# Attention and two mixture layers on one core: order of GpSimd's and TensorE's work within a head step

## The chip, the cores and the metric

The kernel runs on one core of a Trainium2 chip. What is measured is the time of one execution on the device in microseconds (us). TensorE is called PE, its weight loads PEld, VectorE DVE, ScalarE ACT, GpSimd POOL and SyncE, which issues most transfers, SP.

## The reference

Three layers follow one another: attention that keeps the 32 largest scores of each row, a gated layer of width 2048 (called the first layer here, as the kernel's `mm1` and `mm2` are its two products), and a mixture of eight experts with two per token.

```python
scores = q @ k.T / sqrt(64)                       # 4 batches, 8 heads, 576 x 576
kth = the 32nd largest score of each row
attn = softmax(where(scores >= kth, scores, -1e9))
x = attn @ v                                      # 2304 tokens x 512
h = x @ w_in;  x = (h * clip(h + 3, 0, 6) / 6) @ w_out   # w_in 512 x 2048, w_out 2048 x 512, float64
logits = x @ w_gate + log1p(exp(x @ w_noise)) * noise     # the two best of 8 experts
out = sum over the two: weight * (max(x @ w1[e], 0) @ w2[e])
```

## The kernel before, in words

The function `phase_a` does attention, the gated layer and the routing, `phase_b` the experts. Phase A is one long software pipeline over *steps* `st`. A slot is one head for one tile of 128 tokens; there are 144 slots (18 tiles by 8 heads). In each step every stage works on another slot: `scores` of slot st-1, the segment maxima (`seg`) of st-1, the chain that finds the 32nd value (`chain`) and the bias for the exponential (`nbias`) of st-2, `ysum` and `expo` of st-3, `ymax` and `pmask` of st-4, the transposes `ptrans` of st-5, and the products with V (`av`) for a pair of heads, in odd steps, when its second slot is st-6. From step 25 on each step also does one unit of the gated layer: `mm1` of unit u with `hrelu` and `hgate`, and for the unit of the step before (`up`) `hround`, `hlow` and `mm2`. `hlow` makes the lower half of the split value g, on POOL.

The normalisation of a head pair takes three small operations: `recip1` (POOL adds 1e-9 to the two row sums), `recip2` (DVE takes the reciprocal) and `recip3` (POOL spreads the two values over 128 columns, tile `rb`). `av` ends with a transpose of `rb` on PE into the same PSUM bank as the products; ACT copies that bank out two steps after (`xscale`, tile `xs`) and POOL multiplies (`xscale2`).

In the first 21 steps the float64 weights are also converted (`Weights.convert`): DVE shifts bits, ACT scales the low words, and POOL adds the two in place. The order of the first 21 steps is chosen by the framework's scheduler. From step 22 (`KEEP`) on, PE, DVE, ACT and POOL run what `phase_a` issues in exactly the order in which it is written, each engine in its own queue. The routing's indirect transfers (`idw`, 12 for each of the first two groups of tiles) are issued by POOL and are placed by the scheduler, each behind a given `hlow`. Further loads that POOL and ACT share a part of: `q_split` (lower half of q, tile `qsb`) in every second even step, and `k_split` (tile `ksb`) in eight steps ahead of each batch.

Names in the rows: `sum` is the pair of row sums, `a` the bias, `xs`, `xT` the attention values, `g` and `y` as above, `s`, `h`, `pa`, `qp`, `xa`, `av` PSUM banks of scores, `mm1`, `ptrans`, transposed q, `mm2`, and products with V, `e` the exponentials. A helper issues everything in phase A, so all its rows have line 87.

Of the kernel before, what the change touches and what calls it, by code (L numbers as in the profile page):

```python
# [13 lines left out]
ALU = mybir.AluOpType  # L14
# [21 lines left out]
OS, OA, OB, OC, OD, OE, OV, OX, OY = 1, 1, 2, 3, 4, 5, 6, 8, 10  # L36
# [24 lines left out]
def pieces(t):  # L61
    r0 = t * 128
    res = []
    row = 0
    while row < 128:
        b, s = divmod(r0 + row, S)
        n = min(128 - row, S - s)
        res.append((b, row, n, s))
        row += n
    return res  # L70
# [39 lines left out]
class Weights:  # L110
# [27 lines left out]
    def convert(self, fb):  # L138


        if not self.f64:
            return
        nc, t = self.nc, self.raws[fb]
        if self.small:
            m = self.ap.tile([128, 1024], F32, name=f"wm{fb}", tag="wm", bufs=1)
            nc.vector.tensor_scalar(m.bitcast(I32), t[:, :, 1], 0x7FFFFFFF, None, op0=ALU.bitwise_and)
            nc.vector.tensor_scalar(m, m, TINY, None, op0=ALU.is_ge)
        for i in range(2):
            hi = t[:, 512 * i:512 * i + 512, 1]
            tmp = self.ap.tile([128, 512], I32, name=f"wt{fb}_{i}", tag="lx", bufs=LXB)  # L150
            nc.vector.tensor_scalar(tmp, hi, 3, 0x3FFFFFF8, op0=ALU.logical_shift_left, op1=ALU.bitwise_and)
            nc.vector.scalar_tensor_tensor(hi, hi, -0x40000000, tmp, op0=ALU.bitwise_and, op1=ALU.bitwise_or)
        lo = t[:, :, 0]
        nc.scalar.activation(lo, lo.bitcast(U32), AF.Copy, scale=2.0 ** -29)
        nc.gpsimd.tensor_tensor(t[:, :, 1], t[:, :, 1], t[:, :, 0], op=ALU.add)
        if self.small:

            nc.vector.tensor_tensor(t.bitcast(F32)[:, :, 1], t.bitcast(F32)[:, :, 1], m, op=ALU.mult)
# [18 lines left out]
def phase_a(tc, pools, ident, q, k, v, w_in, w_out, X, worst, wscr, stream, begin, on_chunk=None, slots=NSLOT, pace=None):  # L177
    nc = Lanes(tc)
# [35 lines left out]
    def w_split(fb):  # L214
        if fb in stream:
            w = wp.tile([128, 2, 1024], F32R, name=f"wsp{fb}", tag="ws", bufs=NSTR)
        else:
            w = wp.tile([128, 2, 1024], F32R, name=f"w{fb}", tag="wr", bufs=NRES)
            wres[fb] = w
        wk.split(fb, w, fb % 16 < WP)  # L220
        if fb in stream:
            nc.sync.dma_start(wscr[fb], w.bitcast(F32))

    def copy(kind, out, in_):
        (nc.vector.tensor_copy if kind in ONV else nc.scalar.copy)(out, in_)
# [12 lines left out]
    def k_load(i):  # L238
        dl, b, h = ksched[i]
        KR[i] = kr = ap.tile([128, 5, 64], F32, name=f"kr{i}", tag="kr", bufs=KRB)  # L240
        nc.sync.dma_start(kr[:, 0:4, :], k[b, h, 0:512, :].rearrange("(p j) d -> p j d", j=4))
        nc.sync.dma_start(kr[0:64, 4, :], k[b, h, 512:576, :])

    def k_split(i):

        kr = KR.pop(i)
        KS[i] = ks = ksb[i % KSB]
        for sl in ((slice(0, 128), slice(0, 4)), (slice(0, 64), slice(4, 5))):
            hi, lo = ks[sl[0], sl[1], 0, :], ks[sl[0], sl[1], 1, :]
            copy('k', hi, kr[sl])  # L250
            nc.gpsimd.tensor_tensor(lo, kr[sl], ks.bitcast(F32)[sl[0], sl[1], 0, :], op=ALU.subtract)
# [44 lines left out]
    def q_load(t, g):  # L296
        QR[t, g] = qr = ap.tile([128, 4, 64], F32, name=f"qr{t}_{g}", tag="qr", bufs=QRB)
        for (b, row, n, s0) in pieces(t):
            nc.sync.dma_start(qr[row:row + n], q[b, 4 * g:4 * g + 4, s0:s0 + n, :].rearrange("h s d -> s h d"))
# [50 lines left out]
    def seg(i, j):  # L350
        nc.vector.max(ST[i][:, j, :], SS[i][:, edge[j]:edge[j + 1]])
# [12 lines left out]
    def nbias(i):  # L364
        a = A8[i]
        nc.gpsimd.tensor_scalar(a[:, 24:25], a[:, 16:17], -0.125, 1.0, op0=ALU.mult, op1=ALU.mult)
# [45 lines left out]
    def recip1(p):  # L412
        nc.gpsimd.tensor_scalar(SUM[p], SUM[p], 1e-9, 1.0, op0=ALU.add, op1=ALU.mult)

    def recip2(p):
        nc.vector.reciprocal(SUM[p], SUM[p])

    def recip3(p):
        r = SUM.pop(p)
        rb = ap.tile([128, 2, 64], F32, name=f"rb{p}", tag="rb", bufs=2)  # L420
        nc.gpsimd.tensor_scalar(rb, r[:, :, None].to_broadcast([128, 2, 64]), 1.0, 1.0, op0=ALU.mult, op1=ALU.mult)
        RB[p] = rb
# [29 lines left out]
    def av(p):  # L452

        t = p // 4
        AVP[p] = o = ps.tile([128, 512], F32, name=f"av{p}", tag="av")
        for b, row, n, s0 in pieces(t):
            for j in range(5):
                for hh in (1, 0):
                    half = slice(64 * hh, 64 * hh + 64)
                    vt, pt = V[b, (2 * p + hh) % 8][:, j, :], PT[2 * p + hh][:, j, :] if j < 4 else PH[p]  # L460
                    nc.tensor.matmul(o[half, row:row + n], vt, pt[:, row:row + n], start=(j == 0),
                                     stop=(j == 4), skip_group_check=True)
        nc.tensor.transpose(o[:, 128:256], RB.pop(p).rearrange("p a b -> p (a b)"), ident)
# [6 lines left out]
    def xscale2(p):  # L470
        xs = XR.pop(p)
        nc.gpsimd.tensor_tensor(xs[:, 0:128], xs[:, 0:128], xs[:, 128:256], op=ALU.mult)
        XS[p] = xs[:, 0:128]
# [96 lines left out]
    for c, ts in enumerate(chunks):  # L570
        st = max(8 * ts[-1] + 7 + LAG, last + 1)
# [7 lines left out]
    ok = lambda i: 0 <= i < slots  # L579
# [4 lines left out]
    for st in range(-6, end):  # L584
        if st == -6: q_load(0, 0)
        if st == BEGIN: begin()
        if st == KEEP: nc.keep()
        if st % 4 == 0 and 0 < st // 4 + 1 < slots // 4: q_load(*divmod(st // 4 + 1, 2))
        for i, (dl, b, h) in enumerate(ksched):
            if max(dl - 4, min(i, 2) - 6) == st: k_load(i)  # L590
        for fb in wstep.get(st + 2, []): wk.load(fb)

        while fetched < len(units) and units[fetched][0] <= st + 3:
            w_fetch(units[fetched][1]); fetched += 1
        u, up = ustep.get(st), ustep.get(st - 1)
        s_, a, b, c, d, e, av_, x1, x2 = (st - x for x in (OS, OA, OB, OC, OD, OE, OV, OX, OY))
        ki = kdl.get(st)

        if up:
            hround(up)  # L600
            hlow(up)
        if ok(s_):
            scores(s_)
            s_evac(s_)
        if ok(c):
            ysum(c)
            expo(c)
        if ok(d - 1) and d % 2 == 0: recip1(d // 2 - 1)
        if u:
            mm1(u)  # L610
            hrelu(u)
        if ok(e):
            ptrans(e)
            ptevac(e)
        if ki is not None or ok(st):
            kq_trans(ki, st if ok(st) else None)
        if ok(st): q_evac(st)
        if ok(x1) and x1 % 2 == 0: xscale(x1 // 2)

        ch = chain(b) if ok(b) else []  # L620
        segs = [(a, j) for j in range(NSEG)] if ok(a) else []
        if ok(d): ymax(d)
        if ok(d - 1) and d % 2 == 0: recip2(d // 2 - 1)
        if ch:
            ch.pop(0)()
            nbias(b)
        while ch:
            if segs: seg(*segs.pop(0))
            ch.pop(0)()
        if segs: seg(*segs.pop(0))  # L630
        if u: hgate(u)
        if ok(b): zmask(b)
        if ok(d):
            pmask(d)
        while segs: seg(*segs.pop(0))

        if ok(d - 1) and d % 2 == 0: recip3(d // 2 - 1)
        if ok(x1) and x1 % 2 == 0: xscale2(x1 // 2)
        if up:
            mm2(up)  # L640
            if up[1] == NFB - 1: xout(up[0])
        if ki is not None:
            k_trans(ki)
            k_evac(ki)
        if ok(av_) and av_ % 2: av(av_ // 2)
        for i, (dl, b, h) in enumerate(ksched):
            if dl + VL == st: v_load(i)
        if ok(x2) and x2 % 2 == 0: xsplit(x2 // 2)
        if st % 4 == 2 and 0 <= st // 4 + 1 < slots // 4: q_split(*divmod(st // 4 + 1, 2))
        for i, (dl, b, h) in enumerate(ksched):  # L650
            if max(dl - 2, min(i, 2) - 5) == st: k_split(i)
        for fb in wstep.get(st, []): w_split(fb)
        for fb in wstep.get(st + 1, []): wk.convert(fb)
        room = NFILL if st < slots + OD else 3 * NFILL
        while fill and room > 0:
            room -= fill[0][0]
            fill.pop(0)[1]()
# [669 lines left out]
```

## Time and profile before

| | |
|---|---|
| runs | 1385.82 us median of 3 (1384.4 to 1390.74) |
| profiled execution | 1381.3 us, of which the span from first to last instruction is 1379.5 us |
| mean granted TensorE clock | 0.975 of full speed |
| busy in the span | PE 1293.2, PEld 1121.2, DVE 948.3, POOL 829.9, ACT 770.2 us |

The profiled execution is one of its own, 4.5 us (0.3%) below the median of the runs shown. Busy times are averages over stages that differ: the first 145 us (weights and first slots), the head steps up to about 810 us, and what follows on PE.

### The profile page before, as it was taken

How to read it: one execution, taken by the hardware profiler on the slowest of the kernel's cores; microseconds unless marked ns; L12 is line 12 of the kernel's file. 1: busy time of each engine (PE TensorE's matmuls, PEld its weight loads, DVE VectorE, ACT ScalarE, POOL GpSimd, SP SyncE). 2: the span in 40 equal slices, each digit the busy share in tenths (PEclk: the TensorE clock that was granted, in tenths of full speed). 3: DMA queues.
4: the chain of work that ended last, by engine and by line, in shares of the span. 5: the costliest groups of instructions: out<-in, count | busy, mean ns of one | idle time of the engine just before them, and what ended most of it. 6: DMA issues, size and time to landing. Idle time of an engine off the chain costs nothing. (4 is left out here: it accounts for less than half of the span.)

```text
span 1379.5 us, 27084 instructions
## 1 busy us (share of the span) xinstructions
PE 1293.2 (94%) x9006; PEld 1121.2 (81%) x9006; DVE 948.3 (69%) x3560; ACT 770.2 (56%) x1709; POOL 829.9 (60%) x1159
## 2 busy tenths in 40 slices
PE   5878899999999989999999899899999999999996
PEld 3554689989888878898988688788988898898985
DVE  7999987899987978869989753446353545435241
ACT  6888777777778666777777554534322322222220
POOL 7666777677767786767687845133324547465451
PEclk9789999999999999999999999999999999999999
DMA  7776644545365353445544447846446556465431
GB/s 249 261 279 226 230 145 157 193 166 176 132 206 166 127 149 124 170 131 187 175 143 157 123 154 246 265 140 221 136 153 195 178 167 204 140 214 177 137 109 38
DMA packets 138100, 239.56 MB, mean 174 GB/s; under 512 B 39779, under 2 KB 93155, under 8 KB 123872
## 3 DMA queue, kind: packets, MB, share of 16 engines
q1 hardware_dynamic: 127600, 210.57, 46.1%
q0 software_dynamic: 10352, 27.18, 5.9%
q8 instruction: 73, 1.20, 0.4%
q14 instruction: 75, 0.61, 0.2%
HBM read 209.08 MB, written 31.64 MB: 174 GB/s over the span
## 5 line engine op out<-in xcount | busy, mean ns | idle before, releaser
L959 PE MATMUL ac<-w,hh 128*128 128x512 f32 x960 | 247.8, 400 | 1.6 <-ACT hh L941 1.5
L935 PE MATMUL hb<-xe,w 128*128 128x320 f32 (+2 forms) x1536 | 239.4, 311 | 1.0 <-DVE hh L942 0.5
L935 PEld LDWEIGHTS hb<-xe,w 128*128 128x128 f32 x1536 | 232.1, 189 | 10.0 <-issue 3.9
L87 DVE MAX8 seg<-ss 128x8 f32<-128x82 f32 (+1 forms) x1008 | 213.9, 231 | 4.1 <-ACT ss L87 3.7
L87 POOL TENSOR_TENSOR y<-z,ss 128x576 f32<-128x576 bf16 x144 | 205.3, 1426 | 11.7 <-DVE z L87 10.1
L941 ACT ACTIVATE hh<-hb 128x640 fp32r<-128x640 f32 (+2 forms) x72 | 46.6, 647 | 295.7 <-PE hb L935 295.7
L959 PEld LDWEIGHTS ac<-w,hh 128*128 128x128 f32 x960 | 172.8, 188 | 40.3 <-ACT hh L941 5.4
L942 DVE SCALAR_TENSOR_TENSOR hh<-hb,hh 128x640 fp32r<-128x640 f32 (+2 forms) x72 | 53.9, 749 | 213.2 <-ACT hh L941 213.2
L87 PE MATMUL h<-xT,ws 128*128 128x256 f32 x1188 | 159.1, 283 | 9.3 <-DVE r L87 7.9
L87 ACT COPY ss<-s 128x576 f32<-128x576 f32 x144 | 92.6, 643 | 134.6 <-DVE e L87 69.6
L87 PE MATMUL xa<-ws,g 128*128 128x512 f32 x594 | 163.9, 410 | 2.2 <-POOL g L87 0.9
L87 PEld LDWEIGHTS h<-xT,ws 128*128 128x128 f32 x1188 | 150.0, 190 | 12.8 <-DVE r L87 9.9
L921 POOL TENSOR_TENSOR w<-r,w 128x1024 fp32r<-128x1024 f32 x40 | 97.9, 2452 | 85.2 <-ACT w L919 73.4
L87 DVE SCALAR_TENSOR_TENSOR e<-ss,t,e 128x576 f32<-128x576 f32 x144 | 147.6, 1025 | 0.1
L87 POOL TENSOR_TENSOR g<-r,g 128x256 fp32r<-128x256 f32 x124 | 100.2, 808 | 39.8 <-issue 19.6
L87 PEld LDWEIGHTS xa<-ws,g 128*128 128x128 f32 x594 | 104.0, 190 | 23.6 <-POOL g L87 5.1
L87 DVE TENSOR_SCALAR_CACHE_REDUCE z<-ss,a 128x576 bf16<-128x576 f32 x144 | 115.8, 804 | 0.2
L87 ACT ACTIVATE e<-ss,a 128x576 f32<-128x576 f32 x144 | 110.6, 768 | 1.4 <-POOL a L87 1.4
L87 PE MATMUL s<-kt,qt 128*128 128x288 f32 x512 | 101.2, 321 | 7.8 <-ACT qt L87 6.8
L87 DVE MAX8 t<-y 128x8 f32<-128x584 f32 x144 | 107.8, 749 | 0.0
L975 POOL DMA_INDIRECT out_dram<-y,id x40 | 41.8, 1045 | 108.9 <-DVE y L974 86.7
L87 PE MATMUL pa<-ident,e 128*128 128x128 f32 x576 | 91.3, 283 | 15.4 <-DVE e L87 13.4
(427 smaller groups left out, 2617.2 us busy)
## 6 DMA issues: line engine op xcount, KB each, us to landing
ws<-wscr SPq DMA_DIRECT2D x99, 1024.0 KB, 4.8
r<-in_moe_w_dram SPq DMA_DIRECT2D x144, 256.0 KB, 3.1
wscr<-wsp SPq DMA_DIRECT2D x11, 1024.0 KB, 5.8
wraw<-in_moe_w_in_dram SPq DMA_DIRECT2D x16, 512.0 KB, 4.2
wraw<-in_moe_w_out_dram SPq DMA_DIRECT2D x16, 512.0 KB, 5.1
ck<-in_moe_w_in_dram SPq DMA_DIRECT2D x32, 256.0 KB, 3.4
ck<-in_moe_w_out_dram SPq DMA_DIRECT2D x32, 256.0 KB, 3.2
out_dram<-zero SPq DMA_DIRECT2D x18, 256.0 KB, 4.2
```

The costliest lines, as they stand in the source:

```text
L87: o = f(*args, **kw)
L921: eng.tensor_tensor(w[:, 1], r, w.bitcast(F32)[:, 0], op=ALU.subtract)
L935: o = nc.tensor.matmul(p[:, half, 0:hn], w[:, a, d, :], XE[job][:, b, d, half * hn:(half + 1) * hn], start=(m == 0), stop=(m == 11))
L941: nc.scalar.activation(hv[:, 0], p[:, 0:nh, 0:hn], AF.Relu)
L942: LOW[:] = [STT(hv[:, 1], p[:, 0:nh, 0:hn], 0.0, h.bitcast(F32)[:, :, 0:n].rearrange("p a (b n) -> p a b n", b=nh)[:, 0], op0=ALU.max, op1 ...
L959: o = nc.tensor.matmul(ACC[job, j], h[:, a, j * 128:(j + 1) * 128], w[:, b, :], start=(x % NF2 == 0 and m == 0), stop=(x % NF2 == NF2 - 1 ...
L975: s = nc.gpsimd.indirect_dma_start(out=out, out_offset=bass.IndirectOffsetOnAxis(ap=t.bitcast(I32)[:, j, 1:2], axis=0), in_=y, in_offset=N ...
```

## The change

Four things are written in another order or another size; no arithmetic changes. (1) POOL's addition in `convert` is done in four pieces of 256 columns. (2) `recip2` moves in DVE's step from behind `ymax` to the end. (3) `recip3` moves from the end of the even step to the following odd step, behind `ysum`. (4) `nbias` moves to the end of POOL's part of the step, and `av` moves in front of `mm2`.

```diff
-        nc.gpsimd.tensor_tensor(t[:, :, 1], t[:, :, 1], t[:, :, 0], op=ALU.add)
+        for i in range(0, 1024, 256):
+            nc.gpsimd.tensor_tensor(t[:, i:i + 256, 1], t[:, i:i + 256, 1], t[:, i:i + 256, 0], op=ALU.add)
...
         if ok(d - 1) and d % 2 == 0: recip1(d // 2 - 1)
+        if ok(d - 2) and d % 2: recip3(d // 2 - 1)
         if u:
             mm1(u)
...
         if ok(d): ymax(d)
-        if ok(d - 1) and d % 2 == 0: recip2(d // 2 - 1)
         if ch:
             ch.pop(0)()
-            nbias(b)
...
         while segs: seg(*segs.pop(0))
-        if ok(d - 1) and d % 2 == 0: recip3(d // 2 - 1)
+        if ok(d - 1) and d % 2 == 0: recip2(d // 2 - 1)
         if ok(x1) and x1 % 2 == 0: xscale2(x1 // 2)
+        if ok(av_) and av_ % 2: av(av_ // 2)
         if up:
             mm2(up)
...
-        if ok(av_) and av_ % 2: av(av_ // 2)
...
             if max(dl - 2, min(i, 2) - 5) == st: k_split(i)
+        if ok(st - OB): nbias(st - OB)
```

On POOL, an even step and the following odd one (units 8 and 9 of a block of the gated layer) stand like this before:

```order
L87 TENSOR_TENSOR y_8598<-z_8557,ss_8419 128x576
L87 TENSOR_SCALAR sum_8477<-sum_8477 128x2
L87 TENSOR_SCALAR a_8636<-a_8636 128x1
L87 TENSOR_SCALAR rb_8657<-sum_8477 128x128
L87 TENSOR_TENSOR xs_8634<-xs_8634 128x128
L87 TENSOR_TENSOR xT_7971<-xs_8458,xT_7971 128x128
L87 TENSOR_TENSOR qsb_112<-qr_1_8407,qsb_112 128x4x64
L87 TENSOR_TENSOR g_9_8678<-r_9_8616,g_9_8678 128x256
L87 TENSOR_TENSOR y_8689<-z_8651,ss_8508 128x576
L87 TENSOR_SCALAR a_8721<-a_8721 128x1
```

And the same steps on POOL in the changed kernel:

```order
L87 TENSOR_TENSOR y_8646<-z_8604,ss_8467 128x576
L87 TENSOR_SCALAR sum_8523<-sum_8523 128x2
L87 TENSOR_TENSOR xs_8682<-xs_8682 128x128
L87 TENSOR_TENSOR xT_8016<-xs_8506,xT_8016 128x128
L87 TENSOR_TENSOR qsb_112<-qr_1_8455,qsb_112 128x4x64
L87 TENSOR_SCALAR a_8684<-a_8684 128x1
L87 TENSOR_TENSOR g_9_8724<-r_9_8664,g_9_8724 128x256
L87 TENSOR_TENSOR y_8735<-z_8697,ss_8554 128x576
L87 TENSOR_SCALAR rb_8740<-sum_8523 128x128
L87 TENSOR_SCALAR a_8769<-a_8769 128x1
```

The bias `a` now stands behind `qsb`, directly ahead of the next `g`, and `rb` has moved from ahead of `xs` to behind the odd step's `g` and `y`.

On PE, the odd step of that pair before (ten products with V, of which the first and the last stand here):

```order
L87 MATMUL h_10_8694<-xT_6467,ws_10_8409 128x256 x12
L87 MATMUL qpNone_8716<-identr,qsb_111 128x128 x2
L87 MATMUL xa_7963<-w_1219,g_9_8678 128x512 x3
L87 MATMUL xa_7967<-w_1219,g_9_8678 128x512 x3
L87 MATMUL av_8747<-pt_8627,v_7246 64x128
...
L87 MATMUL av_8747<-ph_8625,v_7159 64x128
L87 MATMUL av_8747<-ident,rb_8657 128x128
L87 MATMUL s_8770<-kt_6464,qt_8719 128x288 x4
```

And in the changed kernel:

```order
L87 MATMUL h_10_8742<-xT_6512,ws_10_8457 128x256 x12
L87 MATMUL qpNone_8764<-identr,qsb_111 128x128 x2
L87 MATMUL av_8788<-pt_8675,v_7291 64x128
...
L87 MATMUL av_8788<-ph_8673,v_7206 64x128
L87 MATMUL av_8788<-ident,rb_8740 128x128
L87 MATMUL xa_8008<-w_1247,g_9_8724 128x512 x3
L87 MATMUL xa_8012<-w_1247,g_9_8724 128x512 x3
L87 MATMUL s_8818<-kt_6509,qt_8767 128x288 x4
```

The products with V and the transpose of `rb` now stand between the transposed q and the second product of the gated layer, which with the next scores is queued behind them.

On DVE, from the end of an odd step into the even one, before:

```order
L87 SCALAR_TENSOR_TENSOR e_8334,sum_8477<-ss_8243,t_8115,e_8334 128x576
L87 MAX seg_8510<-ss_8508 128x8 x2
L87 MAX t_8115<-y_8511 128x8
L87 RECIPROCAL sum_8477<-sum_8477 128x2
L87 MAX a_8636<-seg_8510 128x8
L87 MAX seg_8597<-ss_8595 128x8
```

And in the changed kernel, the end of the even step:

```order
L87 TENSOR_SCALAR z_8697,low<-ss_8554,a_8684 128x576
L87 SCALAR_TENSOR_TENSOR e_8560,sum_8699<-ss_8374,t_8163,e_8560 128x576
L87 MAX seg_8645<-ss_8643 128x8 x2
L87 RECIPROCAL sum_8523<-sum_8523 128x2
L87 MAX t_8163<-y_8646 128x8
```

The reciprocal of the same pair now comes almost a whole step later on DVE, behind that step's `hgate`, `z` and `e`.

## Rows read from the trace of the kernel before

**Rows 1.** Busy time in four stretches: start:end, length, PE PEld DVE ACT POOL, PEclk, DMA, GB/s

```profile
50.00:100.00 50.00, 37.65 (x241) 26.78 (x240) 49.28 (x186) 42.09 (x87) 33.85 (x45) 0.86 0.76 269
300.00:350.00 50.00, 50.00 (x414) 45.09 (x413) 45.40 (x211) 36.42 (x92) 34.10 (x52) 1.00 0.49 164
1050.00:1100.00 50.00, 49.91 (x283) 44.58 (x282) 21.88 (x43) 13.72 (x18) 25.36 (x17) 1.00 0.48 155
```

**Rows 2.** Waits from 150 to 800 us: waiter, releaser: us in total, times, longest

```profile
DVE sum L87 <- POOL sum L87: 89.0, 60, 4.8
POOL xs L87 <- ACT xs L87: 67.9, 54, 2.4
...
PEld xa L87 <- POOL g L87: 6.0, 17, 1.3
```

**Rows 3.** Timeline, PE, scores two steps apart: start, us, instruction [idle before <-releaser]

```profile
291.14 0.69 PE L87 MATMUL s<-kt,qt 128*128 128x288 f32 x4
...
300.69 0.56 PE L87 MATMUL s<-kt,qt 128*128 128x288 f32 x3
```

**Rows 4.** Timeline, POOL, a pair of steps with q_split

```profile
308.91 0.30 POOL L87 TENSOR_SCALAR rb<-sum 128x128 f32<-128x128 f32 x1
...
311.19 1.25 POOL L87 TENSOR_TENSOR qsb<-qr,qsb 128x256 fp32r<-128x256 f32 x1
312.40 0.73 POOL L87 TENSOR_TENSOR g<-r,g 128x256 fp32r<-128x256 f32 x1
313.09 1.30 POOL L87 TENSOR_TENSOR y<-z,ss 128x576 f32<-128x576 bf16 x1
314.36 0.20 POOL L87 TENSOR_SCALAR a<-a 128x1 f32<-128x1 f32 x1
```

**Rows 5.** Timeline, PE's weight loads, the odd step of that pair

```profile
312.70 0.30 PEld L87 LDWEIGHTS xa<-ws,g 128*128 128x128 f32 x2
313.18 0.77 PEld L87 LDWEIGHTS xa<-ws,g 128*128 128x128 f32 x4 [0.19 <-POOL g L87]
314.31 0.85 PEld L87 LDWEIGHTS av<-pt,v 128*64 128x64 f32 x16 [0.37 <-issue]
...
315.56 0.14 PEld L87 LDWEIGHTS av<-ident,rb 128*128 128x128 f32 x1 [0.17 <-issue]
```

**Rows 6.** Timeline, DVE, the even step of that pair

```profile
308.40 0.17 DVE L87 RECIPROCAL sum<-sum 128x2 f32<-128x2 f32 x1 [0.48 <-POOL sum L87]
...
310.98 0.86 DVE L87 SCALAR_TENSOR_TENSOR e<-ss,t,e 128x576 f32<-128x576 f32 x1
```

**Rows 7.** Timeline, PE's weight loads, two pairs in a stretch of k_split

```profile
210.01 0.30 PEld L87 LDWEIGHTS xa<-w,g 128*128 128x128 f32 x2
210.63 0.77 PEld L87 LDWEIGHTS xa<-w,g 128*128 128x128 f32 x4 [0.32 <-POOL g L87]
...
221.59 1.23 PEld L87 LDWEIGHTS xa<-ws,g 128*128 128x128 f32 x6
```

**Rows 8.** Timeline, POOL, the same two pairs

```profile
210.54 1.28 POOL L87 TENSOR_TENSOR y<-z,ss 128x576 f32<-128x576 bf16 x1
...
221.93 1.28 POOL L87 TENSOR_TENSOR y<-z,ss 128x576 f32<-128x576 bf16 x1
```

**Rows 9.** Timeline, DVE, first stretch of the routing's indirect transfers

```profile
501.89 0.17 DVE L87 RECIPROCAL sum<-sum 128x2 f32<-128x2 f32 x1 [4.79 <-POOL sum L87]
...
514.52 0.17 DVE L87 RECIPROCAL sum<-sum 128x2 f32<-128x2 f32 x1 [2.83 <-POOL sum L87]
```

**Rows 10.** Timeline, PE, the same stretch

```profile
503.87 0.58 PE L87 MATMUL h<-xT,ws 128*128 128x256 f32 x1 [3.34 <-DVE r L87]
```

**Rows 11.** Timeline, POOL, the same stretch: two transfers and what follows

```profile
502.67 0.44 POOL L87 TENSOR_TENSOR xs<-xs 128x128 f32<-128x128 f32 x1
...
505.27 1.37 POOL L813 DMA_INDIRECT idw<-pl,ix  x1 [0.15 <-issue]
506.95 0.96 POOL L813 DMA_INDIRECT idw<-pl,ix  x1 [0.30 <-DVE t L87]
507.93 1.31 POOL L87 TENSOR_TENSOR y<-z,ss 128x576 f32<-128x576 bf16 x1
```

**Rows 12.** Groups by shape, POOL, 0 to 150 us: busy, mean ns | idle before

```profile
L87 POOL TENSOR_TENSOR wraw<-wraw 128x1024 int32<-128x1024 int32 x16 | 32.7, 2041 | 16.2 <-DVE wraw L87 4.5 <-ACT wsp L87 4.0 <-ACT wraw L87 3.9
```

## The prediction

> **What bounds the kernel now.** I read the busy times by stretch first, then the waits between 150 and 800 us, then single pairs of steps in the timeline. Three stages matter. In the first 145 us DVE is the bound: 49.28 us of 50 while POOL has 33.85 [rows 1]. In the head steps PE has no idle time left in most stretches: 50.00 of 50 us from 300 to 350, PEld 45.09. After 810 us the change moves nothing but the time at which that part starts. So the change is worth what it does to PE between 150 and 800 us, and what it does to DVE before.
>
> In the waits the reader sees a trap. The longest wait of all is that of DVE for POOL's `sum`, 89.0 us in 60 pairs [rows 2], and the change takes it away. But DVE waits there beside a PE that is full. The scores of 291.14 and 300.69 us stand one pair of steps apart, 9.55 us [rows 3], and no weight load in between waits for another engine; this is what a pair costs PE with nothing in its way. Pairs with PE waits are longer, and those waits are short: PEld's `xa` waits for POOL's `g` 6.0 us in 17 places [rows 2]. The exception are the two stretches of POOL's indirect transfers, where PE's `h` idled 3.34 us behind a DVE that had waited 4.79 us [rows 9, 10].
>
> Here the Trainium skill bears, "Perfetto Trace Analysis", section "Identifying the Most-Contended Engine": the matmul row is a poor measure of how full TensorE is, and the share of weight-load time is a better one. By it 45.09 of 50 would leave a tenth free. This trace answers it: from 1050 to 1100 us, where PE's row is as full, PEld has 44.58 of 50 [rows 1]. So I take some 45 as full; what the rule would make of the time is a rival below.
>
> **The change, part by part.** *Four pieces.* 16 additions of 2.04 us [rows 12] become 64 of a quarter. The extra cost is the fixed part of a POOL instruction: `xs` of 128 columns takes 0.44, `g` of 256 takes 0.73 [rows 11, 4], so some 0.15 us is fixed, and 48 more make 7 us. They lie in the first 145 us beside DVE, which is full while POOL has a third of its time free. I cost them at nothing; uncovered they are +7 us. The scheduler also redraws the order of the first 21 steps; DVE has 0.72 us of 50 to lose or gain there, and no other cost shows.
>
> *`recip2` at the end of DVE's step.* The 89.0 us of waiting go. In a pair like that at 308 us the gain for DVE is 0.48 us [rows 6]. What is late next is PE, which was full: I expect DVE to wait for ACT's `r` instead. It costs and gains nothing by itself. It gives DVE and ACT a head start of some tenths on PE.
>
> *`nbias` at the end, `av` ahead of `mm2`.* `xa` gets the time of `av` as extra slack, so its waits for `g` (0.19 us in the pair at 312 us, 0.32 at 210 us [rows 5, 7]) vanish. `nbias` costs `g` its 0.20 us, since it now stands directly ahead of it.
>
> *`recip3` behind the odd step's `y`.* This is the part that costs. PE reaches `av` where it reached `xa` before, and the transpose of `rb` comes as its last instruction; behind it are queued `xa`, the next scores and `mm1`, that is all of PE's work. From the first load of `av` to that of `rb` it is 315.56 - 314.31 = 1.25 us [rows 5]. So PE wants `rb` at 312.70 + 1.25 = 313.95. On POOL `qsb` ends at 312.40; then `nbias` 0.20, `g` (start to start 0.69), `y` (1.27) and `rb` 0.30 [rows 4] put the end of `rb` at 314.86. It is 0.91 us late; less the 0.19 saved, +0.72 us for this pair. Nothing earlier on POOL helps by being shorter: it waits for ACT's `xs`, 67.9 us in 54 pairs [rows 2], so that taking `a` and `rb` away ahead of it only lengthens that wait. Something speaks for less: `qsb` took 1.25 us beside DVE's `e` (310.98 for 0.86 [rows 6]), where `g` of the same size took 0.73, and with the head start `e` is out of its way and ACT's `xs` may come some tenths earlier. The bounds are 0 and 0.91 us late; I take half the net, +0.36.
>
> This holds for pairs with `q_split`. Of 61 pairs in the stretch 12 have `k_split` and 8 indirect transfers; half of the other 41 have `q_split`, and about 6 of those also have the router's transposes on PE, which give `rb` time. That leaves 14: 14 x 0.36 = +5.0 us, bounds -2.7 (only the 0.19 saved) and +10.1. Pairs without `q_split` have 0.7 to 1.2 us less on POOL and I cost them at nothing.
>
> In the 12 pairs with `k_split` POOL has one more stretch ahead of `nbias`. With `q_split`: `y` ends at 211.82, plus 0.20 and 0.30 is 212.32, against 210.01 + 1.25 = 211.26; 1.06 late, 0.74 net. Without: 223.21 + 0.50 = 223.71 against 222.84; 0.87 late and nothing saved [rows 7, 8]. Half again: 6 x 0.37 + 6 x 0.44 = +4.9 us, bounds -1.9 and +9.7.
>
> *Indirect transfers.* A pair there takes 514.52 - 501.89 = 12.63 us [rows 9], 3.08 over PE's 9.55. POOL is the bound: a transfer and the next stand 1.68 and 0.98 us from what follows them [rows 11]. With DVE no longer behind POOL's `sum`, POOL's own waits for DVE shrink, its work doesn't; and two transfers stand between `y` and `rb` in some steps, so that PE waits there for `rb`. I take a third of the 3.08, -1.0 for each of six such pairs: -6 us, bounds -18 and 0.
>
> The sum is +5.0 + 4.9 - 6 = +4 us on the profiled execution's 1381.3, that is 1385.3; that execution stands 4.5 us below the median of the runs shown, so I give 1390 us for the median after.
>
> **The rivals.** *The head start reaches (faster).* If ACT's `xs` comes half a microsecond or more earlier against PE, or POOL's chain from `xs` to `rb` is that much shorter, `rb` is never late; only the saved waits stay (-2.7 and -1.9) and the transfers' stretches give -8: -13, 1373 us. It decides at 0.9 us in the pair at 308 us and 1.06 at 210 us. For it speaks the 0.52 us by which `qsb` was stretched; against it that in the `k_split` pair nothing was stretched and `rb` would still be 1.06 late.
>
> *The full lateness (slower).* POOL's chain keeps its place against PE: +10.1 + 9.7, nothing from the transfers, as `rb` behind two of them (2.66 us) holds PE up: +20, 1406 us. For it speaks that `g` was late for `xa` in 17 places: whenever `g` is just in time, `y` and `rb` after it (1.57 us) come after PE's 1.25.
>
> *No change that can be measured.* PE's 9.55 us holds everywhere, half a wait taken, half a wait given: 1386 us.
>
> *PE has a tenth free.* As a mechanism of this kernel: DVE sets the pair, and the 89.0 us come back until PEld is full, a tenth of 650 us: -65, 1321 us. Against it stands the stretch at 1050 us. The Trainium skill's rule on weight-load share, named above, is what would make it so.
>
> **How the numbers follow.** Chances: the forecast (+4, its own range -3 to +12) 0.48, head start 0.20, full lateness 0.17, no change 0.12, a free tenth 0.03. Half a per cent is 6.9 us, about what this kernel's measurement can tell from nothing. Faster than 1378.9: head start, the free tenth and a trace of the forecast, 0.25. Slower than 1392.7: full lateness and a third of the forecast, 0.34. Same: 0.41. The range 1372 to 1404 leaves out the lower part of the head start's case, the free tenth and the upper half of the full lateness, 2 in 10.
>
> **What the profile after would show.** DVE's waits for `sum` fall from 89.0 us to near nothing, and DVE waits for ACT's `r`. PEld's waits for `g` at `xa` vanish and new ones of `av` for POOL's `rb` appear: 20 us in total is the full lateness, under 3 us the head start. The pair at about 300 us keeps 9.5 us in either case without `q_split`. PE's `h` no longer idles 3 us in the transfers' stretches, where `av` does instead. The first `recip` after 145 us comes within 4 us of where it was. I am wrong if the gain in the transfers' stretches is larger than 8 us, or if the first 145 us change by more than 4.

## The result, and the profile after

The changed kernel takes 1404.89 us (median of 4 runs, 1403.62 to 1406.28); the kernel before took 1385.11 us beside it (median of 4, 1381.61 to 1390.74). The ratio is 1.0139, 95% interval 1.0104 to 1.0175: slower by 19.8 us, just outside the range of the prediction. The profiled execution's span went from 1379.5 to 1402.8 us.

First the waits of the kernel after, from 150 to 800 us, in the columns of [rows 2]: waiter, releaser, us in total, times, longest.

```profile
PEld av L87 <- POOL rb L87: 39.6, 41, 3.6
...
PEld xa L87 <- POOL g L87: 1.0, 4, 0.5
...
POOL xs L87 <- ACT xs L87: 113.6, 56, 3.3
...
DVE seg L87 <- ACT ss L87: 98.0, 75, 4.8
DVE r L87 <- ACT r L87: 12.5, 22, 1.6
```

DVE's wait for `sum` (89.0 us before) is gone, and DVE waits instead for ACT's `ss`, the copy of the scores, which ACT makes when PE has them. PE's weight loads wait for `rb`, in 41 places. `g` is late for `xa` hardly any more (6.0 us before). POOL's wait for `xs` grew by 45.7 us.

The busy times of the same stretches as in [rows 1], in the kernel after:

```profile
50.00:100.00 50.00, 36.35 (x245) 23.82 (x244) 49.39 (x195) 42.70 (x88) 40.13 (x64) 0.96 0.76 273
300.00:350.00 50.00, 48.91 (x405) 45.06 (x406) 42.62 (x204) 36.63 (x91) 32.14 (x52) 1.00 0.48 164
1050.00:1100.00 50.00, 50.00 (x285) 45.10 (x285) 16.87 (x41) 13.48 (x17) 20.43 (x15) 1.00 0.55 177
```

From 300 to 350 us PE has idle time now (50.00 to 48.91), while DVE, which lost its wait, does less in the same time.

**Where the time went.** DVE takes one reciprocal per head pair, 72 in all, and they make a clock for the head steps. I number them from 0. These are the 8th, 13th, 17th, 41st, 45th and 71st of the kernel after, from DVE's timeline:

```profile
147.15 0.14 DVE L87 RECIPROCAL sum<-sum 128x2 f32<-128x2 f32 x1
...
196.40 0.15 DVE L87 RECIPROCAL sum<-sum 128x2 f32<-128x2 f32 x1
...
243.70 0.15 DVE L87 RECIPROCAL sum<-sum 128x2 f32<-128x2 f32 x1
...
500.92 0.15 DVE L87 RECIPROCAL sum<-sum 128x2 f32<-128x2 f32 x1
...
551.03 0.15 DVE L87 RECIPROCAL sum<-sum 128x2 f32<-128x2 f32 x1
...
835.75 0.16 DVE L87 RECIPROCAL sum<-sum 128x2 f32<-128x2 f32 x1
```

So the stretch from 13 to 17, the first with `k_split`, took 243.70 - 196.40 = 47.30 us, and the first with indirect transfers (41 to 45) 50.11; from 8 to 71 it is 688.60 us, against 669.55 before. The table adds such differences for every kernel of this study, each from one profiled execution: *K* is 13 to 17, 33 to 37 and 48 to 52 (the three stretches in which K's heads are split and transposed), *transfers* is 41 to 45 and 65 to 69, *other* is what is left between 8 and 71.

| kernel | 8th at | K | transfers | other | 8 to 71 |
|---|---|---|---|---|---|
| before | 144.63 | 142.5 | 96.7 | 430.3 | 669.6 |
| after | 147.15 | 152.0 | 100.7 | 435.9 | 688.6 |
| recips back | 145.23 | 158.6 | 97.4 | 432.8 | 688.8 |
| av back | 148.58 | 145.3 | 87.5 | 426.0 | 658.8 |
| nbias back | 147.59 | 151.7 | 101.4 | 434.6 | 687.7 |
| four pieces only | 145.44 | 142.5 | 96.7 | 432.0 | 671.2 |
| av behind K's transposes | 147.06 | 146.9 | 102.4 | 434.8 | 684.0 |
| recips back, av behind K's | 145.83 | 144.9 | 96.9 | 433.3 | 675.1 |
| rb's transpose behind mm2 | 147.97 | 146.1 | 88.3 | 427.1 | 661.5 |
| av back, one piece | 147.21 | 145.8 | 90.9 | 426.4 | 663.1 |
| rb ahead of g | 148.99 | 146.3 | 85.9 | 425.6 | 657.8 |
| rb ahead of g, av behind K's | 147.88 | 144.5 | 86.0 | 426.8 | 657.4 |
| av and nbias back | 148.28 | 143.3 | 87.9 | 424.9 | 656.1 |

After less before is +2.5 at the start, +9.5 in K, +4.0 in the transfers, +5.6 in the other pairs, and +1.7 behind the 71st reciprocal (567.05 us to the end of the span, 565.32 before): 23.3 us of span. The sum is right, but two things shift its parts. The reciprocal itself stands almost a step later on DVE, which makes it later at the start and moves time between neighbouring stretches. And DVE can fall behind PE: the reciprocals 28 to 32 of the kernel before are 9.74 to 9.77 us apart, while PE's scores in the same four pairs are 9.54 or 9.55 apart.

So the shares are read once more on PE, from the start of each slot's scores, which the change leaves in their place. They are numbered from 0 to 143; these are the 24th and the 143rd, before and then after:

```profile
154.71 0.79 PE L87 MATMUL s<-kt,qt 128*128 128x288 f32 x4 [1.42 <-ACT qt L87]
...
795.80 0.78 PE L87 MATMUL s<-kt,qt 128*128 128x288 f32 x4
...
154.11 1.33 PE L87 MATMUL s<-kt,qt 128*128 128x288 f32 x4 [1.41 <-ACT qt L87]
...
814.30 0.78 PE L87 MATMUL s<-kt,qt 128*128 128x288 f32 x4
```

Here *K* is 30 to 42, 70 to 82 and 100 to 112, *transfers* is 84 to 98 and 132 to 143, and *other* is what is left between 24 and 143. Other borders move up to some 2.5 us between these columns.

| kernel, by PE's scores | 24th at | K | transfers | other | 24 to 143 |
|---|---|---|---|---|---|
| before | 154.7 | 207.5 | 145.6 | 288.0 | 641.1 |
| after | 154.1 | 218.3 | 147.4 | 294.5 | 660.2 |
| recips back | 156.1 | 226.0 | 145.2 | 288.2 | 659.5 |
| av back | 156.1 | 207.7 | 133.9 | 288.2 | 629.8 |
| four pieces only | 156.2 | 207.5 | 145.6 | 289.0 | 642.0 |
| av behind K's transposes | 154.5 | 210.5 | 150.0 | 294.6 | 655.1 |
| recips back, av behind K's | 156.5 | 211.0 | 144.8 | 290.1 | 645.9 |
| rb's transpose behind mm2 | 155.5 | 210.1 | 134.7 | 287.6 | 632.4 |
| rb ahead of g | 156.3 | 209.8 | 131.8 | 287.4 | 629.0 |
| rb ahead of g, av behind K's | 155.3 | 207.9 | 132.0 | 288.6 | 628.5 |

By this measure after less before is -0.6 at the start, +10.8 in K, +1.8 in the transfers, +6.5 in the other pairs, and +4.8 behind the 143rd scores.

**One pair.** The pair of steps at 315 us of the kernel after has `q_split`; it is of the same kind as that of [rows 4 to 6]. ACT's `qt` and `xs`, DVE's `e`, POOL, and PE's weight loads:

```profile
313.30 0.39 ACT L87 CAST qt<-qpNone 128x256 fp32r<-128x256 f32 x1
313.56 0.41 ACT L87 COPY xs<-av 128x256 f32<-128x256 f32 x1
...
313.81 0.81 DVE L87 SCALAR_TENSOR_TENSOR e<-ss,t,e 128x576 f32<-128x576 f32 x1
...
314.12 0.84 POOL L87 TENSOR_TENSOR xs<-xs 128x128 f32<-128x128 f32 x1 [2.76 <-ACT xs L87]
314.91 0.46 POOL L87 TENSOR_TENSOR xT<-xs,xT 128x128 fp32r<-128x128 f32 x1
315.33 0.74 POOL L87 TENSOR_TENSOR qsb<-qr,qsb 128x256 fp32r<-128x256 f32 x1
316.03 0.19 POOL L87 TENSOR_SCALAR a<-a 128x1 f32<-128x1 f32 x1
316.18 0.73 POOL L87 TENSOR_TENSOR g<-r,g 128x256 fp32r<-128x256 f32 x1
316.88 1.28 POOL L87 TENSOR_TENSOR y<-z,ss 128x576 f32<-128x576 bf16 x1
318.14 0.29 POOL L87 TENSOR_SCALAR rb<-sum 128x128 f32<-128x128 f32 x1
...
316.64 0.85 PEld L87 LDWEIGHTS av<-pt,v 128*64 128x64 f32 x16
317.45 0.25 PEld L87 LDWEIGHTS av<-ph,v 128*64 128x64 f32 x4
318.48 0.14 PEld L87 LDWEIGHTS av<-ident,rb 128*128 128x128 f32 x1 [0.77 <-POOL rb L87]
318.48 1.27 PEld L87 LDWEIGHTS xa<-ws,g 128*128 128x128 f32 x6
```

`rb` ends at 318.43, and PE, which had nothing left of `av`, waits 0.77 us with `xa` behind it. POOL had idled 2.76 us ahead of `xs`: taking `a` and `rb` from that place only lengthened that wait. ACT copies `xs` right behind `qt`, so it can't start before PE has transposed q, whatever DVE does. The stretched instruction has moved, too: `qsb` takes 0.74 us here and not 1.25, as the prediction hoped, but `xs` takes 0.84 beside the same `e` of DVE, where it took 0.46.

PE's scores, two steps apart, show what a pair costs, first one without `q_split` and then this one:

```profile
304.59 0.69 PE L87 MATMUL s<-kt,qt 128*128 128x288 f32 x4
...
314.04 0.69 PE L87 MATMUL s<-kt,qt 128*128 128x288 f32 x4
...
324.09 0.69 PE L87 MATMUL s<-kt,qt 128*128 128x288 f32 x4
```

That is 9.45 and 10.05 us. Before, quiet pairs of either kind take 9.54 to 9.57. So a pair with `q_split` costs 0.5 more, and one without 0.1 less. The 0.37 us by which PE's loads stood idle ahead of `av` ([rows 5]) no longer appear in either.

**The transfers.** The same rows in the first stretch of indirect transfers, POOL and then PE's weight loads:

```profile
528.70 1.29 POOL L87 TENSOR_TENSOR y<-z,ss 128x576 f32<-128x576 bf16 x1
530.14 1.01 POOL L815 DMA_INDIRECT idw<-pl,ix  x1 [0.15 <-issue]
531.46 0.96 POOL L815 DMA_INDIRECT idw<-pl,ix  x1 [0.31 <-issue]
532.44 0.31 POOL L87 TENSOR_SCALAR rb<-sum 128x128 f32<-128x128 f32 x1
...
532.81 0.18 PEld L87 LDWEIGHTS av<-ident,rb 128*128 128x128 f32 x1 [2.59 <-POOL rb L87]
532.81 2.31 PEld L87 LDWEIGHTS xa<-w,g 128*128 128x128 f32 x6
```

Two transfers stand between `y` and `rb`; PE waits 2.59 us here, and up to 3.6 in the pair with the longest wait.

### The profile page after: what moved, and what is told of

It reads as the page before. It is cut to its first block, busy times and chain, and to the rows that moved or that the text cites. A ratio compares the mean times of both kernels' runs of the same rounds, so it can differ in the third digit from the quotient of the medians.

```text
span 1402.8 us, 27182 instructions
## 1 busy us (share of the span) xinstructions
PE 1291.1 (92%) x9006; PEld 1131.1 (81%) x9006; DVE 934.9 (67%) x3560; ACT 770.8 (55%) x1709; POOL 836.4 (60%) x1207
## 5 line engine op out<-in xcount | busy, mean ns | idle before, releaser
L87 POOL TENSOR_TENSOR y<-z,ss 128x576 f32<-128x576 bf16 x144 | 195.3, 1356 | 9.3 <-DVE z L87 6.5
L87 POOL TENSOR_TENSOR xs<-xs 128x128 f32<-128x128 f32 x72 | 52.5, 729 | 132.4 <-ACT xs L87 132.3
L87 DVE SCALAR_TENSOR_TENSOR e<-ss,t,e 128x576 f32<-128x576 f32 x144 | 129.0, 896 | 0.2
L87 PEld LDWEIGHTS xa<-ws,g 128*128 128x128 f32 x594 | 108.4, 196 | 19.2 <-DVE g L87 0.9
L87 POOL TENSOR_TENSOR g<-r,g 128x256 fp32r<-128x256 f32 x124 | 103.7, 836 | 26.6 <-issue 10.4
L87 PE MATMUL s<-kt,qt 128*128 128x288 f32 x512 | 98.6, 317 | 13.5 <-ACT qt L87 11.9
```

The lines of the kernel that those rows point to most:

```text
L87: o = f(*args, **kw)
```

## The experiments

Three theories stood at the start. A: `rb` is late for PE. B: `nbias` at the end of POOL's part makes ACT's exponential late. C: the four pieces and the first 145 us. Later came K: beside A, `av` now stands ahead of K's transposes (`k_trans`), so that ACT's copy `kt` and what ACT has behind it come late. Its rivals are R (K's transposes don't matter), N (`av` ahead of `mm2` is bad by itself) and G (`rb` ahead of `g` makes `g` late). Each ratio is to the kernel before on the same chip; its median there was up to 12 us higher than in the section on the result. The tables above, which stop where the head steps end, are the finer measure: the kernel with the pieces alone agrees with the kernel before to 0.1 us in K and in the transfers.

**The two reciprocal steps back.**

```diff
-        if ok(d - 2) and d % 2: recip3(d // 2 - 1)
...
         if ok(d): ymax(d)
+        if ok(d - 1) and d % 2 == 0: recip2(d // 2 - 1)
...
-        if ok(d - 1) and d % 2 == 0: recip2(d // 2 - 1)
...
+        if ok(d - 1) and d % 2 == 0: recip3(d // 2 - 1)
```

> The changed kernel with recip2 and recip3 alone back at their old places (behind ymax, and at the end of the even step); av stays ahead of mm2, nbias at the end, the four pieces stay. Theory A (rb comes late for the transpose that ends av, since recip3 went back and av went forward): rb is made about two thirds of a step pair earlier, PE's and PEld's waits of av for rb (42.1 us in 42 places after the change) fall under 3 us, DVE's wait for POOL's sum comes back to 70 to 90 us, and the time is 1380 to 1388 us. Theory B (nbias at the end of POOL's step delays ACT's exponential and all behind it): 1398 to 1406 us. Theory C (the four pieces and the first 145 us): 1390 us or more with av's waits gone.

Ratio 1.016 (1.0124 to 1.0196). PE's waits for `rb` are gone and DVE's for `sum` are back (92.3 us from 150 to 800), as A said, but not the time. A alone falls. The time is lost in the K stretches: 158.6 us, 16.1 over the kernel before (18.5 by PE's scores, and next to nothing elsewhere). Rows of this kernel at 204 us: PE, ACT, POOL, DVE.

```profile
201.85 1.80 PE L87 MATMUL av<-pt,v 128*64 128x128 f32 x16
...
204.14 2.25 PE L87 MATMUL xa<-ws,g 128*128 128x512 f32 x6
206.22 0.46 PE L87 MATMUL kp<-identr,ksb 128*128 128x128 f32 x4
...
206.72 0.59 ACT L87 CAST kt<-kp 128x512 fp32r<-128x512 f32 x1 [2.90 <-PE kp L87]
...
207.85 1.01 POOL L87 TENSOR_TENSOR ksb<-kr,ksb 128x256 fp32r<-128x256 f32 x2 [7.54 <-ACT ksb L87]
...
211.27 0.17 DVE L87 RECIPROCAL sum<-sum 128x2 f32<-128x2 f32 x1 [5.14 <-POOL sum L87]
```

PE does `av` and `xa` before K's transposes (`kp`); ACT waits 2.90 us for them with its part of `ksb` queued behind; POOL waits for that 7.54 us; POOL's `sum` is behind it, and DVE waits 5.14 us for `sum`.

**`av` back.** The line of `av` stands behind `mm2` and `k_trans` again, as before the change; the rest of the change stays.

> The changed kernel with av alone back behind mm2. Theory A: PE reaches the transpose of rb by the six xa products (about 1.5 us) later, so the waits of 0.5 to 1.3 us go and those of 2 to 3.6 us in the transfers' stretches shrink to some 1 to 2 us each: av for rb 5 to 12 us in total, xa for g back at 4 to 8 us; the time is 1384 to 1393 us. Theory B: 1398 to 1406 us, since nbias and the reciprocal stay where they are. Theory C: 1390 us or more with av's waits gone.

Ratio 0.9923 (0.9896 to 0.9951): faster than the kernel before. Against the change 29.8 us are saved between 8 and 71. By PE's scores it is 30.4: 13.5 in the transfers, 10.6 in K, 6.3 in the other pairs. Waits from 150 to 800 us:

```profile
PEld xa L87 <- POOL g L87: 11.9, 25, 1.6
PEld av L87 <- POOL rb L87: 5.7, 5, 1.8
```

What is then left of the change gains 10.8 us on the kernel before, 11.3 by the scores, and all of it in the transfers (11.7), where DVE's reciprocal no longer waits for POOL's `sum`. From the 36th to the 72nd scores the two kernels keep the same distance to 0.1 us: outside the transfers the later reciprocal gains PE nothing. B and C fall with this run: `nbias` and the pieces are still as in the change.

**`nbias` back.** The line `nbias(b)` stands behind the first `ch.pop(0)()` again.

> The changed kernel with nbias alone back in the middle of DVE's chain, that is early in POOL's step. Theory A: POOL waits for ACT's xs there, so that the bias costs nothing and g, y and rb come 0.20 us earlier; av's waits for rb fall from 42.1 us by some 6 to 9, and the time is 1394 to 1401 us. Theory B: the exponential gets its bias early, ACT's waits of e for a (14.2 us in 24 places) go, and the time is 1381 to 1389 us. Theory C: 1402 to 1407 us.

Ratio 1.0128 (1.0098 to 1.0157), 687.7 us against 688.6: nothing that can be told. A had expected a gain of 4 to 11 us and overrated the 0.20 us of the bias. The time is one that C had expected, but C falls with the runs above and below.

**The four pieces alone**, in the kernel before.

> The kernel before with the four pieces alone. Theory A and theory B: nothing behind the first 145 us changes, the first reciprocal after 145 us comes 0 to 4 us later, and the time is 1383 to 1389 us. Theory C: 1390 us or more.

Ratio 1.0006 (0.9978 to 1.0034). The 8th reciprocal comes at 145.44 us (144.63 before) and 8 to 71 is 1.6 longer. C falls.

**`av` behind K's transposes** in the steps that have them, everything else as changed.

```diff
-        if ok(av_) and av_ % 2: av(av_ // 2)
+        if ok(av_) and av_ % 2 and ki is None: av(av_ // 2)
...  (behind k_trans and k_evac)
+        if ok(av_) and av_ % 2 and ki is not None: av(av_ // 2)
```

> The changed kernel, but in the steps that transpose a head of K (24 steps, 12 of them with av) av stands behind those transposes and mm2 again; in all others it stays ahead. Theory K (two separate prices of av's move: rb late for it in ordinary pairs, and in the K stretches ACT's copy of kt late because av now stands ahead of K's transposes): the three K stretches (from reciprocal 13 to 17, 33 to 37, 48 to 52) fall from 47.3, 52.8 and 51.9 us to 44.7 to 46.5, 48.5 to 50.5 and 49 to 50; the others keep their length; ratio to the kernel before 1.006 to 1.010. Rival R (rb late is all there is; K's transposes don't matter here): the K stretches lose only the waits of av for rb that stand in them, some 3 us in all, ratio 1.010 to 1.013.

Ratio 1.0144 (1.0106 to 1.0182). K falls by 5.2 us, but 1.1 comes back elsewhere (by PE's scores 7.8 and 2.6, the latter in the transfers). Two of the three stretches are where K put them (46.39 and 49.08), that from 33 to 37 is not (51.38). The ratio is that of neither theory, and the saving doesn't show in it; with DVE free of `sum`, the order against K's transposes costs less than K said.

**Reciprocal steps back, and `av` behind K's transposes.** The two edits together.

> As the kernel with recip2 and recip3 put back (ratio 1.016), with av behind K's transposes and mm2 in the 24 steps that have them. Theory K: that kernel lost its time in the K stretches (49.8, 53.7 and 55.0 us from reciprocal 13 to 17, 33 to 37 and 48 to 52, where the kernel with the pieces alone takes 44.7, 48.2 and 49.6); they return to within 1 us of the latter, ACT's waits of kt for kp of 2.9 us go, and the ratio is 0.997 to 1.004. Rival N (av ahead of mm2 is bad by itself, since it puts ACT and DVE later against PE): the K stretches shrink by less than 2 us each and the ratio stays at 1.010 or above.

Ratio 1.0063 (1.003 to 1.0095). The K stretches return from 158.6 to 144.9, each to 0.5 to 1.5 us above the kernel with the pieces alone, and ACT's waits of `kt` for `kp` fall from 20.7 us (longest 2.9) to 11.6 (longest 1.1). This shows K's mechanism for the old place of the reciprocals: there it was 13.7 (by the scores 15.0) of the 17.6 us by which the kernel lay above that with the pieces alone. The ratio is above K's range; what is left, 3.9 us, is 2.4 in K and 1.3 in the other pairs.

**`rb`'s transpose behind `mm2`.** The last instruction of `av` is issued behind `mm2` and `k_trans`; the products stay ahead.

```diff
-        nc.tensor.transpose(o[:, 128:256], RB.pop(p).rearrange("p a b -> p (a b)"), ident)   # in av
...
+        if ok(av_) and av_ % 2: avt(av_ // 2)     # the same transpose, ahead of v_load
```

> The changed kernel, but the transpose of rb is taken out of av and stands behind mm2 (and K's transposes); the products with V stay ahead of mm2. Theory K: rb is no longer late in ordinary pairs, the waits for rb fall from 42 us to 3 to 8, pairs with q_split go from 10.05 us to 9.5 to 9.6, the transfers' stretches come within 1 us of the kernel with av back (44.2 and 43.3 us from reciprocal 41 to 45 and 65 to 69, against 50.1 and 50.6); the K stretches keep most of their length (ACT's kt still late): ratio 0.995 to 1.002. Rival N: the ratio stays above 1.005, since the products themselves are ahead.

Ratio 0.9945 (0.9912 to 0.9978), just below K's range, 27.1 us less than the change between 8 and 71, from one instruction. The products may stand ahead of `mm2`; N falls. The waits for `rb` are 6.0 us in 4 places.

**`rb` ahead of `g`.** The other side of the same wait: POOL makes `rb` earlier in the odd step, and PE's order stays that of the change.

```diff
+        if ok(d - 2) and d % 2: recip3(d // 2 - 1)
         if up:
             hround(up)
             hlow(up)
...
-        if ok(d - 2) and d % 2: recip3(d // 2 - 1)   # behind ysum
```

> The changed kernel with one line moved: recip3 still in the odd step, but ahead of hround and hlow, so that POOL makes rb before g and y (some 2 us earlier), and before the indirect transfers. Theory K (rb late on POOL is the larger part of the loss, and av ahead of K's transposes the smaller): the waits of av for rb go from 42 us to under 4, the transfers' stretches (reciprocal 41 to 45 and 65 to 69) from 50.1 and 50.6 to 43 to 46 us, pairs with q_split from 10.05 to 9.6 or less, while the K stretches stay 1 to 2 us above those of the kernel with av back; from reciprocal 8 to 71 656 to 664 us instead of 688.6, ratio to the kernel before 0.990 to 0.996. Rival N (the products ahead of mm2 cost time whatever rb does): above 670 us, ratio above 1.000. Rival G (rb ahead of g makes g late for xa): waits of xa for g above 8 us, 665 to 675 us.

Ratio 0.9916 (0.9885 to 0.9946), 657.8 us: 30.8 us less than the change by the place of one line, as K said. Quiet pairs take 9.44 to 9.48 us, with `q_split` or without. The K stretches were to stay 1 to 2 us each above those with `av` back; they stay 1.0 above in all (2.1 by PE's scores), and the first is shorter. Waits of this kernel from 150 to 800 us, and POOL at a pair of transfers:

```profile
PEld xa L87 <- POOL g L87: 8.2, 14, 1.3
...
PEld av L87 <- POOL rb L87: 2.4, 6, 0.9
...
515.42 0.30 POOL L87 TENSOR_SCALAR rb<-sum 128x128 f32<-128x128 f32 x1
515.70 0.73 POOL L87 TENSOR_TENSOR g<-r,g 128x256 fp32r<-128x256 f32 x1
516.39 1.29 POOL L87 TENSOR_TENSOR y<-z,ss 128x576 f32<-128x576 bf16 x1
517.85 1.61 POOL L815 DMA_INDIRECT idw<-pl,ix  x1 [0.16 <-issue]
```

`rb` is now made before `g`, `y` and the transfers; the transfers' stretches are the shortest of all kernels here. `g` is late for `xa` in 14 places, 8.2 us, so G has a part, but it costs less than it brings.

**The same, and `av` behind K's transposes.**

> The same, and in the steps with K's transposes av behind them and mm2. Theory K: the K stretches (13 to 17, 33 to 37, 48 to 52) come down by 1 to 2 us each against the kernel with rb ahead of g alone; from reciprocal 8 to 71 652 to 661 us, ratio 0.987 to 0.994. Rival N or G: no difference to that kernel, or longer.

Ratio 0.9923 (0.9891 to 0.9954), 657.4 us. K falls by 1.8 us in all, not by 1 to 2 in each stretch, and the first of them rose by 1.6. With `rb` in time, the place of `av` against K's transposes is worth nothing that can be told.

**`av` and `nbias` back.**

> The changed kernel with av and nbias both back, so that recip2, recip3 and the four pieces are left of the change. Theory K (nbias is worth nothing either way): from reciprocal 8 to 71 657 to 661 us as with av back alone (658.8), ratio 0.991 to 0.996. Theory B (nbias at the end makes ACT's exponential late, 13 us in 26 places with av back): 650 to 656 us, ratio 0.985 to 0.990, and ACT's waits of e for a gone.

Ratio 0.9934 (0.9902 to 0.9965), in K's range and not in B's; the 656.1 us lie between the two, 0.9 below K's and 0.1 above B's. ACT's waits of `e` for `a` are gone, as B said, but with them `nbias` is worth 2.7 us at most, and not 13.

**`av` back and the addition in one piece.**

> The kernel before with recip2, recip3 and nbias moved as in the change, av behind mm2 and the addition in one piece: the combination that the runs so far point to. Theory K: as fast as the changed kernel with av back, or faster by up to 2 us, as the first 145 us are the old ones: ratio 0.989 to 0.993. Rival (the pieces give something to what follows): 0.994 to 1.000.

Ratio 0.9979 (0.9955 to 1.0003), 663.1 us: slower than K said, and in the range of its rival. It is 4.3 us more than the kernel with four pieces takes, of which 3.4 are in the first transfers' stretch: POOL stood idle for 2.69 us ahead of its first transfer, which comes before `rb`, and PE then waited 3.94 us for `rb`. The transfers stand at the same places of POOL's queue as with four pieces, where POOL idled 0.19 us there. The profile shows nothing that the transfer waited for, so whether the pieces have a part in it stays open. The second transfers' stretch is the same in both (43.3 us).

## Why the prediction was wrong

**The step that failed** is the one on the indirect transfers, "I take a third of the 3.08, -1.0 for each of six such pairs: -6 us". It measured +1.8 by PE's scores (+4.0 by the reciprocals), above even the upper bound, 0. The prediction had named what decides there, that two transfers stand between `y` and `rb`, but neither its forecast nor its bounds hold a cost for it; only the rival of full lateness did, and it set the cost equal to the gain. The gain behind it is real, and larger than foretold: with `rb` in time these stretches give 11.7 us (`av` back) or 13.8 (`rb` ahead of `g`). But `rb` behind two transfers takes 13.5 to 15.6 us; in six pairs PE's loads waited 17 us for it.

**"Half again" in the K stretches** is the second: +4.9 was foretold, +10.8 measured (+9.5 by the reciprocals). Of this 8.5 goes when `rb` is made ahead of `g`, close to the bound of full lateness (+9.7). Half was too little because nothing that spoke for less came true. POOL's chain begins with ACT's `xs`, ACT copies that behind `qt`, and `qt` follows PE: 1.25 us from PE's load of transposed q to ACT's `xs` before (308.54 to 309.79), 1.21 after (312.35 to 313.56). There was no head start on PE to be had. And the 0.52 us by which `qsb` was stretched did not go; 0.38 of it went to `xs`. The other 2.3 us, no more than the choice of borders is worth, are there with `rb` in time too. The prediction did not see that `av` also passes K's transposes: in the changed kernel, putting it behind them takes 7.8 us off K, though the two causes overlap, since with `rb` in time the same edit takes 1.9 off K and 0.5 off the whole.

**The other pairs** came out nearly right, +6.5 for +5.0, and for the reason given: with `rb` in time nothing is left of it (288.0 us before, 288.2 with `av` back, 287.4 with `rb` ahead of `g`). In a quiet pair with `q_split` PE's loads waited 0.77 us where full lateness was 0.91, and the pair cost 0.5 net where the forecast had 0.36 and the bound 0.72. The 0.1 us that `av` ahead of `mm2` gives to pairs without `q_split` was not foreseen, nor that a pair with the router's transposes takes 0.7 us longer by it (11.52 for 10.86 from the 56th to the 58th scores). That the later reciprocal "costs and gains nothing by itself" beside a full PE was right, and so was PE's price of a quiet pair, 9.55 us.

**The four pieces** are right as a whole: the first reciprocal behind 145 us came 2.5 us later (within 4), but that is mostly its own move; PE's 24th scores came 0.6 us earlier. With the pieces alone it is 0.8 and 1.5 us later. Their own cost was mis-sized: POOL's 64 additions took 759 ns each, 47.3 us for 32.7, so 14.6 more and not 7; the cover held. **DVE's wait** for `sum` fell to nothing, and turned up at `ss` (98.0 us) more than at `r` (12.5). **`xa` for `g`** went from 6.0 to 1.0 us. **`nbias`** is as small as costed.

**The rivals.** What happened is nearest to the full lateness, +20 and 1406 us foretold, 1404.9 measured. Its reason held: "whenever `g` is just in time, `y` and `rb` after it come after PE's 1.25". That the sum agrees so well is in part luck: the K term was 1.1 us too low with a second cause in it, the other pairs 3.6 too high, and the nothing from the transfers (+1.8) is a gain and a loss of 12 us and more. The head start (-13) is about what the kernels with `rb` in time show, -6.5 to -13.5 us between 8 and 71, but they have it from the transfers, where it had -8; its condition was not met by the change. A free tenth of PE never showed: with `rb` ahead of `g` PEld is at 45.35 of 50 us between 300 and 350, where it had been at 45.09.

Not settled: what POOL's first transfer in the kernel with one piece waited for, and why the part behind the last scores took 4.8 us longer in the profiled execution after.

## What to carry to other kernels

An operand that one engine makes last and another wants last is priced on both queues at once: count from a common event (here PE's transposed q) to the end of the producer's chain and to the consumer's last instruction. When the producer's chain starts behind a wait for the consumer's own engine, nothing that is moved out of it ahead of that wait shortens it, so expect more than half of the lateness: here 0.5 of 0.72 us in a quiet pair and 8.5 of 9.7 in the K stretches. Work of another kind that stands ahead of the late operand, here two transfers, needs a term of its own. A gain and a loss can sit in the same edit set: here the reciprocal's new time was worth 11 us and the place of one POOL line took 31 (by PE's scores); before dropping such a change, move the late operand ahead of the long work in the producer's step (0.9916). And read the price of a stage on the engine that bounds it: between DVE's reciprocals a quiet pair seemed to gain 0.2 us by `av` back (from 9.75 to 9.55), between PE's scores it gained nothing (9.54 and 9.55).

## What the runs showed of the hardware that was not expected

The stretch beside DVE's `e` went from one POOL instruction to another: before, `qsb` took 1.25 us behind an `e` that had begun 0.21 us earlier (0.74 without one); after, `xs` took 0.84 behind one that had begun 0.31 us earlier (0.46 without). From 150 to 800 us the mean of `qsb` fell from 0.94 to 0.73 us, and that of `xs` rose from 0.55 to 0.77. The Trainium skill, "SBUF — State Buffer", section "Who interferes with whom", says that a DVE instruction with two inputs in SBUF contends with a GpSimd instruction that reads SBUF, and that the order of issue decides which of the two blocks. `e` reads two tiles in SBUF, and the trace agrees: `e` began first, and `xs` ended at 314.96, behind the end of `e` at 314.62. It also shows what followed for this schedule: the shift of DVE against POOL didn't remove the stretch, it gave it to the neighbour.

Behind the 143rd scores the change alters little by design, yet that part took 583.7 us before, 588.5 after, and 595 to 610 us in the profiled executions of the experiments. Spans of single executions could not have told these kernels apart; the stretches between scores could.
